# Attention loads paced along the preceding batch, last six outputs scaled by ScalarE, and a replanned order

## The chip, the cores and the metric

The kernel runs on one core of a Trainium2 chip. The core has five engines that run side by side, each with its own queue of instructions: TensorE (PE, matrix products; its weight loads are shown as PEld), VectorE (DVE), ScalarE (ACT), GpSimd (POOL) and SyncE (SP), which here only issues DMAs. The metric is device time in microseconds of one execution; less is better.

## What is computed

Block-sparse attention for 4 batches, 8 heads, 768 positions and 64 channels a head, followed by a two-layer block over the 3072 rows of 512 channels:

```python
scores = scale * np.matmul(q, k.transpose(0, 1, 3, 2))
scores = np.where(mask, scores, -1000000000.0)      # first, last, neighbour and sampled blocks
attn = np.exp(scores - max) / sum
x = (attn @ v), rows (batch, position), columns (head, channel)
h = x @ w_in                                         # 512 -> 1024
solu = h * softmax(h)
ln = (solu - mean) / np.sqrt(var + 1e-06) * g_ln
out = ln @ w_out                                     # 1024 -> 512
```

## The kernel before

The mask enters as 24 further channels of queries and keys (one for each block of 32 positions), so that one matrix product of 88 channels gives masked scores. Scores are computed with the keys along the partitions; the row sum of the exponentials comes out of the value product through a column of ones in `va`.

**Attention.** A unit is (batch b, tile t of 256 queries, pair pr of heads): 4 x 3 x 4 = 48 units. Each has three groups of four score matmuls (`score`, L495) into a PSUM bank group `sbank`, three exponentials on ScalarE (L502) into `ex`, three groups of eight value matmuls (`pv`, L512) into one of two small banks `mbank`, and on VectorE a reciprocal (L523) and a scaling (L526) into `x`. There are three `sbank`s; from batch 1 on, two serve scores and one the dense layers.

**Feed.** When the four pairs of a tile are done, its 256 rows go through the dense layers in two halves a = 0, 1. `x` is transposed (by a DMA transpose on SP, L556, or by TensorE for the first and last tile), then: eight matmuls with `w_in` (`hmm`, L567), an exponential with row sums on ScalarE (L576), the product h * exp on VectorE (L580, called `so`), centring (L584, `ce`), statistics (L587, L590), an inverse root on GpSimd (L592 to L598), a transpose of the centred rows (L606, or by TensorE), eight matmuls with `w_out` (`outp`, L613) into an `mbank`, a scaling of the result by the inverse root (`fin`, L623) into `ot`, and a store on SP (L629).

**Loads.** Keys, queries and values come in by pairs of heads, 384 KB a load, on SP (`load`, L270), into four staging buffers each. From batch 1 on, keys and queries are cast on GpSimd (L417), transposed by a DMA on SP (L422) and copied to `kT` and `qT` by VectorE (L427); values are cast by GpSimd (L477). Loads, transposes and stores all stand on the one queue of SP, in order: a transpose that waits for its cast holds back every load behind it.

**The order.** No loop issues the work. Every piece is made as an `Op` with an engine, an assumed duration, what it depends on (`deps`), what it must merely be planned after (`after`), buffers to take, and a due time; lists `A` (units), `F` (feeds), `Q` (preparation of heads) and `SHIFT` hold the due times. `Plan.run` then lays all ops out on the engines with a model of durations and DMAs, and the program is emitted in that order. On the chip only the order on each engine's queue is kept, and the waits that the data call for. The plan's own times are not used in what follows.

Of the kernel before, what the change touches and what calls it, by code (L numbers as in the profile page):

```python
# [12 lines left out]
ACT = mybir.ActivationFunctionType  # L13
# [9 lines left out]
def act_us(n, sbuf=False):  # L23
    return (n + 60 + (52 if sbuf else 0)) / 1200
# [31 lines left out]
class Plan:  # L56


    def __init__(self):
        self.ops = []  # L60
        self.pools = {}
        self.free = {e: 0.8 for e in SEEN}
        self.dma_free = 0.0
        self.xbar_free = 0.0
        self.landed = []

    def pool(self, name, n, of=None, first=0):
# [3 lines left out]
    def op(self, eng, us, emit, deps=(), due=0.0, take=None, last_of=(), load=None, after=()):  # L71
        o = Op(eng, us, emit, deps, due, take, last_of, load, after)
        for d in {id(d): d for d in o.deps + o.after}.values():
            d.next.append(o)
            o.open += 1
        for a, name in o.last_of:
            a.held[name][0] += 1
        self.ops.append(o)
        return o

    def run(self):
        ready = {e: [] for e in SEEN}

        def enter(o):
            o.at = max([0.0] + [d.seen for d in o.deps] + [d.start for d in o.after])
            ready[o.eng].append(o)

        for o in self.ops:
            if not o.open:
                enter(o)  # L90
        order = []
        while len(order) < len(self.ops):
            best = None
            for e, ops in ready.items():
                now = self.free[e]
                for o in ops:
                    t = o.at
                    for name in o.take:
                        free, ids = self.pools[name]
                        t = max(t, min(free[k] for k in ids))  # L100
                    if t == INF:
                        continue
                    late = t > now + 0.02
                    key = (t if late else now, o.due)
                    if best is None or key < best[0]:
                        best = (key, o, max(t, now))
            assert best is not None, "nothing can be placed"
            _, o, t = best
            ready[o.eng].remove(o)
            us = o.us * (2 if o.eng == "PE" and t < COLD else 1)  # L110
            self.free[o.eng] = t + us
            o.start = t
            o.seen = t + us + SEEN[o.eng]
            if o.load is not None and o.xbar:
                self.xbar_free = max(self.xbar_free, t + 1.0) + o.load * (1.4 if self.dma_free > t + 1 else 1.0)
                self.dma_free = max(self.dma_free, t) + o.load
                o.seen = self.xbar_free + 1.3
            elif o.load is not None and o.eng != "SP":
                o.seen = t + (2.8 if o.load > 0.1 else 2.0) + o.load + 0.6 * min(o.load, max(0.0, self.dma_free - t - 1.5))
                if o.load > 0.1:  # L120
                    self.dma_free = max(self.dma_free, t + 1.5) + o.load
            elif o.load is not None:
                self.dma_free = max(self.dma_free, t + 1.0) + o.load
                o.seen = self.dma_free + 1.0
                self.landed.append(self.dma_free)
                if len(self.landed) > 6:
                    self.free["SP"] = max(t + o.us, self.landed[-7])
            for name in o.take:
                free, ids = self.pools[name]
                o.slots[name] = min(ids, key=lambda k: (free[k], k))  # L130
                free[o.slots[name]] = INF
            for a, name in o.last_of:
                held = a.held[name]
                held[0] -= 1
                held[1] = max(held[1], o.seen)
                if not held[0]:
                    self.pools[name][0][a.slots[name]] = held[1]
            order.append((t, len(order), o))
            for n in o.next:
                n.open -= 1  # L140
                if not n.open:
                    enter(n)
        order.sort(key=lambda r: r[:2])
        return [o for _, _, o in order]
# [3 lines left out]
def kernel(  # L148
# [13 lines left out]
    B, H, S, D = q.shape  # L162
# [7 lines left out]
    NPR = H // 2  # L170
# [57 lines left out]
    plan = Plan()  # L228
# [5 lines left out]
    plan.pool("h", 1, "sh", 2)  # L234
    op = plan.op
    LOAD = 2 * P * NCH * D * 4 / 330e3
    TILE = 0.023

    def bank(o, dt=FP32):
        t = mbank[o.slot]  # L240
# [6 lines left out]
        return sbank[o.slot].rearrange("p a b -> p (a b)")  # L247

    def xbar_us(tiles):
        return 1.35 if tiles < 64 else 1.5  # L250


    samp_i = const.tile([NB, NR, 2], I32, name="samp_i")
# [11 lines left out]
    stage, loads = {}, []  # L265
# [40 lines left out]
    mid, stz, last = fill(ident, 0.0, -2198), fill(static, 0.0, -2197), fill(anyeq, 0.0, -2196)  # L306

    def sel(t, us, fill, base, cm, pat, deps, cmp=ALU.is_ge):
# [7 lines left out]
            due=-2194)  # L316
# [8 lines left out]
    for r in range(NR):  # L325
        last = op("DVE", 0.24, lambda o, r=r: nc.vector.scalar_tensor_tensor(
            out=anyeq, in0=kbi, scalar=samp_i[:, r, 0:1], in1=anyeq, op0=ALU.is_equal, op1=ALU.max),
            [last, io, samp_dma], due=-2089)
# [3 lines left out]
    def selq_tr(o):  # L332
        for c in range(NCH):
# [5 lines left out]
             due=-2189, last_of=[sqt])  # L339
# [5 lines left out]
               due=-2079.6)]  # L345
# [24 lines left out]
    for i in (1, 2, 0):  # L370
# [8 lines left out]
                due=-1900 if i == 0 else 0) for i in range(2)]  # L379
# [5 lines left out]
    w_out_load = []  # L385
    for i in range(3):
        w_out_load.append(op("SP", 0.5, lambda o, i=i: nc.sync.dma_start(
            out=hold[i], in_=moe_w_out.rearrange("(c p) d -> p c d", p=P)[:, 3 * i : min(3 * i + 3, KF)]),
            due=-43.4 + 0.1 * i, load=2.3, deps=w_in_load[:1], after=[stage[("v", 0, 3)]] + w_out_load[-1:]))
    stage[("k", 1, 0)].after.append(w_out_load[-1])  # L390
    w_out_load[-1].next.append(stage[("k", 1, 0)])
    stage[("k", 1, 0)].open += 1
    gt = op("PE", 0.1, lambda o: nc.tensor.matmul(bank(o)[:, 0:KF], g8, identf[0:KF, 0:KF], start=True, stop=True),
            [g_load, idf, stage[("k", 0, 2)]], due=15, take="m")
    gc = op("DVE", 0.1, lambda o: nc.vector.tensor_copy(out=g_sb, in_=bank(gt)[:, 0:KF]), [gt], due=15,
            last_of=[gt])
# [88 lines left out]
    def attend(b, t, pr, A):  # L485
# [4 lines left out]
        for n in range(3):  # L490
            def score(o, n=n):
                s = sbank[o.slot]
                for m in range(4):
                    hh, jc = divmod(4 * n + m, NCH)
                    nc.tensor.matmul(s[:, m, :], kT[i][0:DM, pr, hh, jc * P : (jc + 1) * P],  # L495
                                     qT[i][0:DM, pr, hh, t * TW : (t + 1) * TW],
                                     start=(m % 2 == 0), stop=(m % 2 == 1))

            so = op("PE", 4 * 0.1087, score, need[0] + (need[1] if n else []), due=A + 0.9 * n,
                    take="sh" if b == 0 and t < 2 else "s")  # L500
            last_use.setdefault((b, pr), []).append(so)
            exs.append(op("ACT", act_us(1024), lambda o, so=so: nc.scalar.activation(  # L502
                out=exb[o.slot], in_=sbank[so.slot], func=ACT.Exp, scale=scale), [so], due=A + 0.9 * n,
                take="ex", last_of=[so]))
        pv0 = None
        for n in range(3):
            def pv(o, n=n, pv0=pv0):
                acc = bank(pv0 or o)[:, 0 : 4 * (D + 1)].rearrange("p (a h d) -> p a h d", a=2, h=2)
                for m in range(4):
                    hh, jc = divmod(4 * n + m, NCH)  # L510
                    for qt in range(2):
# [6 lines left out]
                     last_of=[exs[n]], after=[pv_last] if n else [])  # L518
# [12 lines left out]
            take="x" if fresh else None, last_of=[pv0, rc])  # L531
# [17 lines left out]
    def feed(b, t, F, by_pe, late):  # L549
# [10 lines left out]
        for a in range(2):  # L560
            h0 = None
            for n in range(4):
                def hmm(o, n=n, h0=h0, a=a):
                    h = pair(h0 or o)
                    f = n // 2
                    for c in (2 * (n % 2), 2 * (n % 2) + 1):
# [5 lines left out]
                       take=None if n else ("sh" if late else "h"), last_of=[xp] if n == 3 else [],  # L572
# [10 lines left out]
                last_of=[h0, (se, "e")])  # L583
# [14 lines left out]
            rs = op("POOL", 0.55, lambda o, mv=mv: nc.gpsimd.tensor_tensor(  # L598
                out=rsb[o.slot], in0=mvb[mv.slot][:, 0:1], in1=neg_half, op=ALU.pow), [q2, nh],
                due=F[a] - 30, take="rs", last_of=[mv])  # L600
# [24 lines left out]
                else:  # L625
                    nc.scalar.activation(out=otb[o.slot], in_=bank(o0), func=ACT.Copy, scale=rsb[rs.slot])

            fo = op("DVE", 0.74, fin, [om, rs], due=F[a] + 7, take="ot", last_of=[o0, rs])
            op("SP", 0.45, lambda o, a=a, fo=fo: nc.sync.dma_start(  # L629
                out=out_v[b, 2 * t + a], in_=otb[fo.slot]), [fo], due=F[a], last_of=[fo], load=0.8)  # L630

# [1 line left out]
    units += [(b, t, pr) for b in range(1, B) for t in range(NT) for pr in range(NPR)]  # L633


    A = [-45.65, 40.00, 223.39, 84.45, 113.83, -10.10, 148.66, 400.63, 32.23, 154.32, 246.42, 58.30, -154.55,
         -261.32, -38.68, -86.73, -83.04, -37.93, -122.58, -397.07, -7.44, 96.20, 125.06, 92.18, -24.08,
         -186.30, 68.39, -9.13, -331.82, 0.92, 45.16, -14.53, -5.50, 84.85, 136.68, 26.21, 15.45, 11.53,
         -92.83, -240.79, 14.95, 126.21, -14.78, 139.91, -324.93, 225.39, 184.04, 142.76]
    F = [-252.59, -78.30, 47.15, -69.94, -182.12, -193.82, 100.11, -114.06, 22.11, -50.57, -74.19, -53.05,  # L640
         275.34, -203.17, 194.98, -23.42, -88.40, 56.44, 21.43, 55.08, 340.35, 167.71, 248.37, 18.28]
    Q = [-252.59, 107.13, -181.40, 669.66, 579.50, 93.95, 204.07, 225.32, 34.97, -16.48, 130.68, -51.20,
         -335.57, -838.94, -885.84, -745.64]
    for b in range(B):
        for pr in range(NPR if b == 1 else 0):

# [11 lines left out]
            j = b * NT + t  # L658
            feed(b, t, F[2 * j : 2 * j + 2], j in (0, B * NT - 1), j >= B * NT - 3)

    SHIFT = {"score": -3.8, "hmm": 113.54, "outp": 336.1, "pv": -218.66}
    for o in plan.ops:
        o.due += SHIFT.get(o.emit.__name__, 0.0)

# [42 lines left out]
```

## Time and profile before

| | |
|---|---|
| Median of 13 runs | 214.19 us (212.82 to 219.13) |
| The profiled execution, its own time | 212.82 us |
| Its span, from first to last instruction | 210.8 us |
| DMA | 41.28 MB, mean 196 GB/s |
| Exponentials of attention (L502) | 144, 1043 ns each, 137.2 us in all |
| Scalings of the output (L623) | 24, 748 ns each, 18.0 us in all |
| Products of the dense layer (L580) | 24, 1222 ns each, 29.3 us in all |
| Landing of a load of keys, queries, values | 5.1, 5.4, 4.5 us (median) |
| Landing of a DMA transpose of keys, queries, x, centred rows | 4.2, 3.9, 3.6, 3.7 us (median) |

The busy times of the engines overlap. Matmuls are pipelined, so a matmul's own duration in the table of groups is longer than the time from one to the next. In a few places a matmul's record is missing from the trace; weight loads are complete, and the starts of blocks are read from them.

### The profile page before, as it was taken

What the parts mean: (1) busy time and instruction counts of PE and PEld (TensorE: products, weight loads), DVE (VectorE), ACT (ScalarE), POOL (GpSimd) and SP (SyncE); (2) the same over time, 40 slices, a digit from 0 to 9 for tenths busy, and PEclk for the clock granted to TensorE, in tenths of its full rate; (3) what the DMA queues carried; (4) which work ended last, traced back from release to release, by engine and by line L of the source; (5) the groups of instructions that cost most, each with busy time, mean ns of one, the idle gap of its engine ahead of it and who ended that gap; (6) DMA issues with size and microseconds to landing.
All of it is one profiled execution on the core that took longest, in us unless ns stands there. A gap on an engine that the chain in (4) does not pass through costs nothing.

```text
span 210.8 us, 5781 instructions
## 1 busy us (share of the span) xinstructions
PE 198.6 (94%) x2269; PEld 141.6 (67%) x2298; DVE 161.9 (77%) x379; ACT 165.6 (79%) x202; POOL 63.4 (30%) x131
## 2 busy tenths in 40 slices
PE   7899999989999999999999999999999999999981
PEld 6589878857667777666677777667665566644430
DVE  4797998747995986985856675894848797789882
ACT  6699999988998899999799889699955688743000
POOL 5143026333642462246243111233011112121120
PEclk9999999999999999999999999999999999999999
DMA  5999998999999998999999952543674755325522
GB/s 176 317 384 344 263 314 210 214 260 279 257 207 214 301 235 174 306 206 331 227 317 237 245 98 65 89 115 87 96 158 100 127 124 101 96 50 155 151 103 100
DMA packets 69119, 41.28 MB, mean 196 GB/s; under 512 B 52188, under 2 KB 64484, under 8 KB 69092
## 3 DMA queue, kind: packets, MB, share of 16 engines
q1 hardware_dynamic: 68496, 39.86, 77.0%
q0 software_dynamic: 544, 1.05, 2.6%
q8 instruction: 18, 0.29, 0.6%
q14 instruction: 9, 0.07, 0.1%
q10 hardware_dynamic: 52, 0.00, 0.0%
HBM read 23.07 MB, written 6.29 MB: 139 GB/s over the span
## 4 chain that ended last, share of the span: by engine, by line
PE 74%; ACT 10%; DVE 4%; DMA 4%; issue 3%; SPq 2%; POOL 0%; ACTq 0%; DVEq 0%; POOLq 0%
PE sbank L495 24%; PE mbank L613 17%; PE sbank L567 17%; PE mbank L512 13%; ACT ex L502 10%; DMA kb<-kb 2%; DMA qst<-in_q_dram 2%; SPq L270 2%; DVE ot L623 1%; PE mbank L459 1%; DVE kT L427 1%; PE mbank L542 1%; DVE bn L587 1%; ACT eso L576 0%; DVE qT L427 0%
## 5 line engine op out<-in xcount | busy, mean ns | idle before, releaser
L502 ACT ACTIVATE ex<-sbank 128x1024 bf16<-128x1024 f32 x144 | 137.2, 1043 | 11.6 <-PE sbank L495 10.8
L495 PE MATMUL sbank<-qT,kT 88*128 88x256 bf16 x576 | 81.8, 272 | 3.2 <-ACT ex L502 2.1
L495 PEld LDWEIGHTS <-kT 88*128 88x128 bf16 x576 | 52.6, 97 | 23.7 <-issue 7.2
L567 PE MATMUL sbank<-w_in_sb,xT 128*128 128x512 bf16 x174 | 47.9, 379 | 0.8
L613 PE MATMUL mbank<-w_out_sb,eso 128*128 128x512 bf16 x181 | 45.6, 379 | 1.7 <-DVE ot L623 1.2
L512 PEld LDWEIGHTS <-ex 128*128 128x128 bf16 x1152 | 42.4, 98 | 6.6 <-DVE x L526 0.2
L512 PE MATMUL mbank<-va,ex 128*128 128x65 bf16 x1152 | 44.0, 193 | 0.1
L580 DVE SCALAR_TENSOR_TENSOR eso<-sbank,eso 128x1024 bf16<-128x1024 f32 x24 | 29.3, 1222 | 10.8 <-ACT eso L576 10.8
L576 ACT ACTIVATE eso<-sbank 128x1024 bf16<-128x1024 f32 x24 | 24.8, 1031 | 15.3 <-issue 3.1
L587 DVE BATCH_NORM_STATS2 bn<-eso 128x6 f32<-128x512 bf16 x48 | 30.7, 682 | 0.2
L613 PEld LDWEIGHTS <-eso 128*128 128x128 bf16 x192 | 18.3, 97 | 18.1 <-issue 1.6
L567 PEld LDWEIGHTS <-xT 128*128 128x128 bf16 x192 | 18.3, 98 | 11.3
L594 POOL TENSOR_SCALAR mv<-se,mv 128x1 f32<-128x1 f32 x24 | 6.9, 288 | 60.3 <-DVE mv L590 54.6
L523 DVE RECIPROCAL r<-mbank 128x4 f32<-128x4 f32 x48 | 8.3, 174 | 17.9 <-PE mbank L512 17.7
L623 DVE TENSOR_SCALAR ot<-mbank,rs 128x512 f32<-128x512 f32 x24 | 18.0, 748 | 5.0 <-PE mbank L613 4.2
L526 DVE TENSOR_TENSOR x<-mbank,r 128x256 bf16<-128x256 f32 x48 | 20.0, 418 | 0.8
L477 POOL CAST va<-vst 128x768 bf16<-128x768 f32 x16 | 13.2, 826 | 16.7 <-DMA vst<-in_v_dram 11.8
L598 POOL TENSOR_TENSOR rs<-mv,neg_half 128x1 f32<-128x1 f32 x24 | 13.9, 579 | 13.0 <-DVE ot L623 11.8
L417 POOL CAST kb<-kst 128x768 bf16<-128x768 f32 x12 | 10.5, 872 | 15.6 <-ACT ex L502 10.7
L417 POOL CAST qb<-qst 128x768 bf16<-128x768 f32 x12 | 10.8, 898 | 12.9 <-DMA qst<-in_q_dram 10.6
L427 DVE COPY kT<-kb 64x768 bf16<-64x768 bf16 x24 | 10.5, 436 | 3.7 <-DMA kb<-kb 2.9
L584 DVE TENSOR_SCALAR eso<-eso,mu 128x1024 bf16<-128x1024 bf16 x24 | 13.2, 548 | 0.1
(72 smaller groups left out, 97.8 us busy)
## 6 DMA issues: line engine op xcount, KB each, us to landing
vst<-in_v_dram SPq DMA_DIRECT2D x16, 384.0 KB, 4.5
out_dram<-ot SPq DMA_DIRECT2D x24, 256.0 KB, 2.3
kst<-in_k_dram SPq DMA_DIRECT2D x15, 384.0 KB, 5.1
qst<-in_q_dram SPq DMA_DIRECT2D x15, 384.0 KB, 5.4
w_in_sb<-in_moe_w_in_dram POOLq DMA_DIRECT2D x2, 512.0 KB, 11.5
kT<-in_moe_w_out_dram SPq DMA_DIRECT2D x1, 768.0 KB
qT<-in_moe_w_out_dram SPq DMA_DIRECT2D x1, 768.0 KB, 16.1
eso<-in_moe_w_out_dram SPq DMA_DIRECT2D x1, 512.0 KB
```

What stands on the lines that cost most here:

```text
L417: nc.gpsimd.tensor_copy(out=half(cb[o.slot], 0).rearrange("p (c h d) -> p c h d", c=NCH, h=2), in_=st[ld.slot].rearrange("p h c d -> p c h ...
L495: nc.tensor.matmul(s[:, m, :], kT[i][0:DM, pr, hh, jc * P : (jc + 1) * P], qT[i][0:DM, pr, hh, t * TW : (t + 1) * TW], start=(m % 2 == 0), ...
L502: exs.append(op("ACT", act_us(1024), lambda o, so=so: nc.scalar.activation(out=exb[o.slot], in_=sbank[so.slot], func=ACT.Exp, scale=scale) ...
L512: nc.tensor.matmul(acc[:, qt, hh, :], exb[exs[n].slot][:, m, qt * P : (qt + 1) * P], va[i][:, 2 * pr + hh, jc, :], start=(n + m + qt == 0) ...
L526: nrm = op("DVE", 0.41, lambda o: nc.vector.tensor_tensor(out=xb[x_of[(b, t)].slot][:, :, 2 * pr * D : (2 * pr + 2) * D].rearrange("p a (h ...
L567: nc.tensor.matmul(h[:, f * 512 : (f + 1) * 512], xTb[xp.slot][:, a, c, :], w_in_sb[:, c, f * 512 : (f + 1) * 512], start=(c == 0), stop=( ...
L576: se = op("ACT", act_us(d_ff) + 0.22, lambda o, h0=h0: nc.scalar.activation(out=eb[o.slots["e"]], in_=pair(h0), func=ACT.Exp, accum_out=se ...
L580: so = op("DVE", 1.3, lambda o, h0=h0, se=se: nc.vector.scalar_tensor_tensor(out=sob[o.slot], in0=pair(h0), scalar=1.0, in1=eb[se.slots["e ...
L587: bn = op("DVE", 2 * 0.68, lambda o, so=so: [nc.vector.bn_stats(out=bnb[o.slot][:, f], in_=sob[so.slot][:, f * 512 : (f + 1) * 512]) for f ...
L598: rs = op("POOL", 0.55, lambda o, mv=mv: nc.gpsimd.tensor_tensor(out=rsb[o.slot], in0=mvb[mv.slot][:, 0:1], in1=neg_half, op=ALU.pow), [q2 ...
L613: nc.tensor.matmul(bank(o0 or o), sotb[st.slot][:, f, :], w_out_sb[:, f, :], start=(f == 0), stop=(f == KF - 1))
L623: nc.vector.tensor_scalar(out=otb[o.slot], in0=bank(o0), scalar1=rsb[rs.slot], scalar2=None, op0=ALU.mult)
```

## The change

Four things. In the model of the plan, DMA transposes and loads share one DMA queue, where transposes had one of their own, and SP is held up by them in another way; the assumed costs of a transpose change with it. Each load of batches 2 and 3 is planned after the first score group of one unit of the batch before (twelve loads, twelve units). The scaling of the last six outputs is given to ScalarE. And the due times `A`, `F`, `Q` and `SHIFT` are new, so that the order differs on every engine from the first blocks on. The instructions are otherwise the same ones, with the same shapes.

```diff
+    def follow(self, o, d):
+
+        o.after.append(d)
+        d.next.append(o)
+        o.open += 1
...
-            if o.load is not None and o.xbar:
-                self.xbar_free = max(self.xbar_free, t + 1.0) + o.load * (1.4 if self.dma_free > t + 1 else 1.0)
-                self.dma_free = max(self.dma_free, t) + o.load
-                o.seen = self.xbar_free + 1.3
-            elif o.load is not None and o.eng != "SP":
+            if o.load is not None and o.eng != "SP":
...
             elif o.load is not None:
-                self.dma_free = max(self.dma_free, t + 1.0) + o.load
-                o.seen = self.dma_free + 1.0
+
+                before, last = self.dma_free, self.xbar_seen
+                self.dma_free = max(before, t + 1.0) + o.load
+                o.seen = self.dma_free + 0.9
                 self.landed.append(self.dma_free)
+                if o.xbar:
+                    self.free["SP"] = max(t + us, last - 1.5, before - 4.0)
+                    self.xbar_seen = o.seen
...
-    TILE = 0.023
+    TILE = 0.0245
...
-        return 1.35 if tiles < 64 else 1.5
+        return 1.24
...
             last_use.setdefault((b, pr), []).append(so)
+            if n == 0 and 1 <= b < B - 1:
+
+                l = NPR * t + pr
+                plan.follow(stage[("kqv"[l % 3], b + 1, l // 3)], so)
...
-            fo = op("DVE", 0.74, fin, [om, rs], due=F[a] + 7, take="ot", last_of=[o0, rs])
+            fo = op("ACT" if late else "DVE", 0.52 if late else 0.74, fin, [om, rs], due=F[a] + 7, take="ot", last_of=[o0, rs])
...
-    A = [-45.65, 40.00, 223.39, 84.45, 113.83, -10.10, 148.66, 400.63, 32.23, 154.32, 246.42, 58.30, -154.55,
+    A = [51.93, 316.63, -115.93, 231.11, 59.19, -252.77, -562.27, -274.63, -180.24, 25.80, 75.07, -201.10,
...
-    SHIFT = {"score": -3.8, "hmm": 113.54, "outp": 336.1, "pv": -218.66}
+    SHIFT = {"score": 83.14, "hmm": 360.52, "outp": 460.27, "pv": -613.9}
```

`late` is true for the three tiles of batch 3, two outputs each. `fin` already held both branches: a multiplication on VectorE, or `nc.scalar.activation` with `Copy` and the inverse root as scale.

## The prediction

> **What bounds the kernel now.** I read the page's engine shares first, then the busy time by windows, then the chain that ended last in order of time, then the timeline of the last stretch. One execution is shown: span 210.8 us, its own time 212.82 us, so 2.0 us lie around the span; the median of 13 runs is 214.19, or 1.4 us more.
>
> Page, shares of the engines:
> ```profile
> PE 198.6 (94%) x2269; PEld 141.6 (67%) x2298; DVE 161.9 (77%) x379; ACT 165.6 (79%) x202; POOL 63.4 (30%) x131
> ```
> Windows (busy us and instruction counts of PE, weight loads, DVE, ACT, POOL; clock; DMA share; GB/s):
> ```profile
> 20.00:30.00 10.00, 9.81 (x154) 8.64 (x153) 8.81 (x22) 10.00 (x12) 0.00 (x0) 1.00 1.08 301
> ...
> 90.00:100.00 10.00, 9.45 (x109) 6.67 (x109) 6.86 (x17) 9.58 (x14) 5.42 (x9) 1.00 1.18 272
> ...
> 130.00:140.00 10.00, 9.89 (x101) 6.68 (x102) 8.39 (x20) 8.13 (x11) 2.49 (x6) 1.00 0.36 57
> ```
> TensorE is busy everywhere at full clock; ScalarE is full only early; the DMA engines are full to about 120 us and a third busy later. A share of 94% does not say how much of TensorE's time is necessary, so I priced its blocks from the dense rows of the chain (start, us, what):
> ```profile
> 17.44 0.75 PE mbank L512 x24
> 18.19 0.88 PE sbank L495 x8
> ...
> 147.41 1.73 PE mbank L613 x8
> ...
> 191.65 1.73 PE sbank L567 x8
> ```
> Dense, a score matmul costs 0.109 us, a value matmul 0.031, a matmul of the two dense layers 0.216, a transpose 0.056. So 576 x 0.109 + 1152 x 0.031 + 384 x 0.2156 + 48 x 0.056 is 183.8, and some 4.6 for the transposes of batch 0: 188.4 us of necessary work. The first score starts at 8.2 and the last matmul ends at 206.4, which is 198.2. TensorE lost about 9.7 us in between, and these alone are to be had, apart from the 4.4 after the last matmul.
>
> To place the loss I took each block's start less 8.1 less the necessary work ahead of it ("lag"). It is 5.0 us at 48 us, 5.6 at 61, 5.9 at 67, 6.7 at 99, 7.1 at 105, 7.85 at 180 and 9.4 at 203. Three causes:
> - To 61 us, ScalarE. It runs 144 exponentials in 137.2 us, 0.953 each, and a score cannot reuse a PSUM bank before its exponential is done. Adding the exponentials up in order against the TensorE work ahead of the first block that needs them, the worst place of the old order is 43 x 0.953 + 1 x 1.24 (an exponential of the dense layer, 1.03 + 0.21) = 42.2 against 37.0 of work: 5.3 us behind. Measured 5.0; VectorE adds the rest by 61.
> - At 99 us, 0.8 us, and 0.3 when it restarts: a late transpose on the queue of SyncE.
> ```profile
> 89.94 0.58 SPq L270
> ...
> 90.57 1.55 SPq L270
> ...
> 92.17 0.47 SPq L270
> ...
> 92.74 4.86 DMA kb<-kb
> ...
> 97.62 0.36 DVE kT L427
> ```
> The last keys of batch 2 wait on SP behind three loads of batch 3 (2.6 us, one stuck 1.55), then 4.86 us for a transpose whose usual landing is 4.2.
> - In the last 15 us, 1.6 us: VectorE holds the two small PSUM banks.
> ```profile
> 201.92 0.75 DVE L623 TENSOR_SCALAR ot<-mbank,rs 128x512 f32<-128x512 f32 x1 [0.25 <-issue]
> 202.59 0.20 DVE L590 BATCH_NORM_AGGREGATE mv<-bn 128x2 f32<-128x12 f32 x1
> 202.71 0.64 DVE L546 COPY eso<-mbank 128x1024 bf16<-128x1024 bf16 x1
> 202.73 3.61 PE L613 MATMUL mbank<-w_out_sb,eso 128*128 128x512 bf16 x16 [0.90 <-DVE ot L623]
> ```
>
> **What the Trainium skill says.** "Perfetto Trace Analysis", Identifying the Most-Contended Engine: matmul occupancy is no measure of headroom, weight-load share is a better one. The trace agrees: 94% against 67%; hence the sum above. "DMA: Bandwidth & Descriptors", Anatomy of one DMA: semaphore waits sit on the issuing sequencer, the DMA engines wait for none; and under Issuing engines are not separate DMA queues: all issuers share the same 16 engines. Both are seen: the rows at 89.94 to 92.74, and queue q1 with 39.86 of 41.28 MB. "ScalarE: Activation LUTs", Table sets: copy is in every table set. The trace has one table load although copies (L342, L354, L467) and exponentials share the engine, so six Copy activations between exponentials should bring none.
>
> **The change part by part.** The count of instructions per engine is the same but for six scalings; all else is order.
>
> 1. New order in the first 60 us. At 48.3 us of work the new order has 53 attention and 3 dense exponentials due: 53 x 0.953 + 3 x 1.24 = 54.2, so 6.0 behind, where the old peak was 5.3. VectorE's own queue, summed the same way from the first product of the dense layer on, asks for 1.5 us beyond its start in the old order and 1.0 in the new. Taking both, lag at 53 us of work is about 6.0 against 5.9 measured before: +0.1, ends 0 and +0.9 (the two shortfalls add up fully).
>
> 2. Pacing. It adds no semaphore: it only sets where a load stands on SP's queue. Counted from the built order, a load of keys or queries of batch 2 or 3 stands at least 20.9 us of TensorE work ahead of the first score that needs it. What it needs: landing 5.4, cast 0.9, issue 1.24, transpose landing 4.2, two copies 0.87, near 12.6. Values have 11.9 and more against 4.5 + 0.83. So the loads are not late, though they now stand behind two transposes and stores of outputs, which wait for VectorE. The transposes of the last keys of batch 2 now stand behind two other transposes and no load, with 10.3 us against 2 x 1.24 + 1.24 + 4.2 + 0.87 = 8.8. The 0.8 + 0.3 stall should go: -1.1, ends -1.1 and 0. Last loads go out nearer 125 us than 115.7; DMA there is idle enough. What is late next: VectorE at 112.8 us of work (0.4 by its queue's sum) and the transpose for batch 3, tile 1 (5.1 us against 0.7 + 3.6 + waits). I take +0.2, ends 0 and +0.8.
>
> 3. Six scalings on ScalarE. They take 6 x 0.748 = 4.5 us off VectorE's last 30 us, where it is 90% busy from 180 to 200, and put them on an engine with 2.2 us of work in 190 to 200 and none after. No row shows a 512-column Copy; between a 256-column copy (0.365) and a 1024-column exponential (1.03), 512 columns give about 0.59; the skill's rule under Rules for kernel authors (0.3 us and 0.83 ns an element) gives 0.73. I take 0.6: the very last scaling gets 0.15 shorter (ends 0 and 0.2). Inside the tail I walked the new order with the durations above: the copy of the first transposed block waits for VectorE, and the scaling of output (3, 2, 0) on ScalarE waits for its inverse root, since its aggregate stands on VectorE behind the last product (1.3 us) and GpSimd adds 0.27 + 0.55 and hops. That bank is wanted by the last transpose. The walk gives 1.7 to 1.9 of stall; the same kind of sum for the old tail gives 2.6 where 1.6 was measured, so it overstates by 1. I take 1.1 against 1.6: -0.5, ends -1.6 and +0.4. Without ScalarE's cover, VectorE would owe the 4.5 us again in the same place.
>
> Sum: +0.1 - 1.1 + 0.2 - 0.5 - 0.15 = -1.45, so 211.4 against 212.82 in its own execution, and 212.7 against the median.
>
> **Rivals.**
> - A deeper gain: the front costs nothing, the tail stall all but goes (-1.6), nothing new appears: -1.1 - 1.6 - 0.15 = -2.85, 211.3. For it: ScalarE lies idle in the tail. Against it: the wait for the inverse root.
> - No change: ScalarE's extra 0.7 at the front stays on, VectorE's 0.4 and the tail at 1.9 appear as summed: +0.7 - 1.1 + 0.4 + 0.3 - 0.15 = +0.15, 214.3. For it: every later stall can only add to a lag that the front already set.
> - Slower: paced loads late. Each store and transpose on SP waits for VectorE, and a load behind it waits along. If that holds a load back by more than the spare 20.9 - 12.6 = 8.3 us, the pair of heads it belongs to starts late. The one late pair above cost 1.1 with its restart; four pairs would cost 4.4 less the gain of 1.45: +2.9, 217.1; three give 216.0. For it: SP waited 12.3 us for VectorE ahead of stores. Against it: the longest single wait there was 3.3 us. I take 216.0 for it.
> - The pacing does nothing: the old queue already trickled its loads out to 115.7 us as buffers came free. Then the gain is that of order alone and falls within the first two cases.
>
> **How the numbers follow.** Forecast 212.7, chance 0.45, its own range 211.7 to 213.5. Deeper gain 0.13. No change 0.20. Slower 0.22. About 0.3%, 0.64 us, is what measurement can tell from no change. Forecast and deeper gain lie below 213.55 but for a little at the edge: faster 0.57; same 0.20; slower 0.23. The range takes in the deeper gain and most of the slower case, and half a microsecond for the scatter of medians: 210.9 to 215.9.
>
> **What would show it.** Lag near 6 us at 60 us of time, as before; no gap on TensorE near 99 us and no transposed keys for which VectorE idles; DMA busy to about 125 us at lower shares; scalings on ScalarE near 0.6 us and no second table load; 1 us or so of gaps in the last 15 us, the last of them ahead of the final transpose. It is wrong if VectorE idles for landed transposes or GpSimd's casts wait for loads in batches 2 and 3, or if ScalarE's lag passes 7 us.

## The result, and the profile after

| | before | after |
|---|---|---|
| Median, run side by side | 214.35 us (212.75 to 220.05, 48 runs) | 211.11 us (210.43 to 214.23, 11 runs) |
| Profiled execution, own time | 212.82 us | 211.43 us |
| Its span | 210.8 us | 209.7 us |
| Time around the span | 2.0 us | 1.7 us |

The ratio of the two is 0.9861, with a 95% interval of 0.9839 to 0.9884: the change takes 1.4% off, about 3.0 us. Ratios here and below leave out disturbed executions, those well above the fastest of their kernel, so a ratio can differ a little from that of two medians. Between the two profiled executions the difference is 1.39 us. Both figures are needed below: the forecast was worked out on the second and carried over to the first.

The page of after, shares of the engines, and its DMA row of 40 slices (tenths, each slice 5.2 us):

```profile
PE 199.0 (95%) x2270; PEld 141.5 (67%) x2298; DVE 157.8 (75%) x373; ACT 169.9 (81%) x208; POOL 63.6 (30%) x131
...
DMA  5999997979994086998989989999790464634522
```

Six instructions went from VectorE to ScalarE: 4.1 us less on the one, 4.3 us more on the other. From the 2nd slice on the DMA engines stay at seven tenths or more to the 30th, 157 us, where the forecast said about 125. The exception is the 13th to the 16th slice, 63 to 84 us, with 4, 0, 8 and 6 tenths: between 54 and 76 us no load goes out.

The same windows as before the change (busy us and counts of PE, weight loads, DVE, ACT, POOL; clock; DMA share; GB/s):

```profile
20.00:30.00 10.00, 9.79 (x144) 8.49 (x142) 8.40 (x20) 10.00 (x12) 0.00 (x0) 1.00 1.09 297
90.00:100.00 10.00, 9.83 (x124) 7.40 (x126) 7.20 (x19) 8.59 (x11) 3.52 (x6) 1.00 1.10 223
130.00:140.00 10.00, 9.89 (x142) 7.43 (x141) 8.11 (x19) 8.75 (x12) 4.54 (x9) 1.00 1.17 261
```

From 90 to 100 us TensorE is busy 9.83 us where it was 9.45: the stall near 99 us is gone. From 130 to 140 us the DMA share went from 0.36 to 1.17 and TensorE did not lose by it: these are the loads that are now paced into the second half.

The last stretch, from the timeline of after (start, us, engine, line, operation):

```profile
201.35 0.69 ACT L635 ACTIVATE ot<-mbank,rs 128x512 f32<-128x512 f32 x1 [1.04 <-PE mbank L622]
...
202.08 0.61 PE L551 MATMUL mbank<-ident,eso 128*128 128x128 bf16 x8
...
202.53 2.92 PE L622 MATMUL mbank<-w_out_sb,eso 128*128 128x512 bf16 x12
202.80 0.69 DVE L555 COPY eso<-mbank 128x1024 bf16<-128x1024 bf16 x1 [0.98 <-PE mbank L551]
```

The scaling of `ot` on ScalarE runs beside VectorE's work, the final transposes start at 202.08 as it ends, and `outp` of the tile before goes on under the copy of the transposed block. No row of TensorE there has an idle time of its own; before, `outp` waited 0.90 us for VectorE's scaling.

With the measure of the prediction, lag (a block's start less the first score's and the necessary work ahead of it), the two profiles compare like this:

| us | before | after | difference |
|---|---|---|---|
| First score starts | 8.11 | 7.75 | -0.36 |
| Lag at 50 us of work | 5.82 | 7.13 | +1.31 |
| Growth, 50 to 180 us of work | 1.87 | 1.45 | -0.42 |
| Growth, 180 to 188 us of work | 1.72 | 0.29 | -1.43 |
| From the last block's start to the end | 5.24 | 5.03 | -0.21 |
| Sum | | | -1.11 |

That is the 1.1 us between the spans; the other 0.3 lies around them. The front got worse by far more than expected, the tail got better by far more, and the middle by less.

The table rests on one execution of each kernel. In two further profiles of the kernel before, the stall in the middle is much larger than the 0.8 us of the first; this is shown with the experiments.

### The profile page after: what moved, and what is told of

The parts are those of the page before. It is cut to its first block, busy times and chain, and to the rows that moved or that the text cites. A ratio compares the mean times of both kernels' runs of the same rounds, so it can differ in the third digit from the quotient of the medians.

```text
span 209.7 us, 5779 instructions
## 1 busy us (share of the span) xinstructions
PE 199.0 (95%) x2270; PEld 141.5 (67%) x2298; DVE 157.8 (75%) x373; ACT 169.9 (81%) x208; POOL 63.6 (30%) x131
## 2 busy tenths in 40 slices
DMA packets 69119, 41.28 MB, mean 197 GB/s; under 512 B 52188, under 2 KB 64484, under 8 KB 69092
## 3 DMA queue, kind: packets, MB, share of 16 engines
q1 hardware_dynamic: 68496, 39.86, 77.1%
## 4 chain that ended last, share of the span: by engine, by line
PE 76%; ACT 11%; DMA 4%; SPq 3%; issue 3%; DVE 2%; ACTq 0%
PE sbank L500 24%; PE mbank L622 19%; PE sbank L576 17%; PE mbank L521 14%; ACT ex L511 9%; DMA kst<-in_k_dram 4%; SPq L277 3%; PE mbank L551 1%; ACT eso L585 1%; DVE w_out_sb L403 1%; PE mbank L464 1%; DVE qT L472 0%; ACT ot L635 0%; DVE kb L446 0%; DVE x L535 0%
## 5 line engine op out<-in xcount | busy, mean ns | idle before, releaser
L500 PE MATMUL sbank<-qT,kT 88*128 88x256 bf16 x576 | 82.9, 272 | 2.5 <-ACT ex L511 1.9
L576 PE MATMUL sbank<-w_in_sb,xT 128*128 128x512 bf16 x177 | 48.6, 379 | 0.6
L521 PEld LDWEIGHTS <-ex 128*128 128x128 bf16 x1152 | 41.7, 97 | 6.6 <-issue 1.4
L521 PE MATMUL mbank<-va,ex 128*128 128x65 bf16 x1152 | 43.1, 193 | 1.2 <-DVE qT L472 0.7
L589 DVE SCALAR_TENSOR_TENSOR eso<-sbank,eso 128x1024 bf16<-128x1024 f32 x24 | 29.3, 1221 | 10.2 <-ACT eso L585 10.0
L585 ACT ACTIVATE eso<-sbank 128x1024 bf16<-128x1024 f32 x24 | 24.8, 1033 | 15.0 <-PE sbank L576 10.5
L603 POOL TENSOR_SCALAR mv<-se,mv 128x1 f32<-128x1 f32 x24 | 7.4, 309 | 61.4 <-DVE mv L599 52.1
L482 POOL CAST va<-vst 128x768 bf16<-128x768 f32 x16 | 13.8, 863 | 17.2 <-DMA vst<-in_v_dram 17.0
L632 DVE TENSOR_SCALAR ot<-mbank,rs 128x512 f32<-128x512 f32 x18 | 13.5, 748 | 4.0 <-PE mbank L622 3.0
L422 POOL CAST kb<-kst 128x768 bf16<-128x768 f32 x12 | 10.5, 873 | 15.6 <-PE mbank L521 10.7
L601 POOL TENSOR_TENSOR se<-se 128x1 f32<-128x1 f32 x24 | 4.8, 200 | 32.1 <-ACT eso L585 32.1
L422 POOL CAST qb<-qst 128x768 bf16<-128x768 f32 x12 | 10.2, 852 | 8.0 <-DMA qst<-in_q_dram 6.5
L593 DVE TENSOR_SCALAR eso<-eso,mu 128x1024 bf16<-128x1024 bf16 x24 | 12.3, 513 | 0.3
```

Source lines behind the costliest of these rows:

```text
L422: nc.gpsimd.tensor_copy(out=half(cb[o.slot], 0).rearrange("p (c h d) -> p c h d", c=NCH, h=2), in_=st[ld.slot].rearrange("p h c d -> p c h ...
L482: vc = op("POOL", pool_us(S) + 0.3, lambda o: nc.gpsimd.tensor_copy(out=va[i][:, 2 * pr : 2 * pr + 2, :, 0:D], in_=vst[ld.slot]), [ld, von ...
L521: nc.tensor.matmul(acc[:, qt, hh, :], exb[exs[n].slot][:, m, qt * P : (qt + 1) * P], va[i][:, 2 * pr + hh, jc, :], start=(n + m + qt == 0) ...
L576: nc.tensor.matmul(h[:, f * 512 : (f + 1) * 512], xTb[xp.slot][:, a, c, :], w_in_sb[:, c, f * 512 : (f + 1) * 512], start=(c == 0), stop=( ...
L585: se = op("ACT", act_us(d_ff) + 0.22, lambda o, h0=h0: nc.scalar.activation(out=eb[o.slots["e"]], in_=pair(h0), func=ACT.Exp, accum_out=se ...
L589: so = op("DVE", 1.3, lambda o, h0=h0, se=se: nc.vector.scalar_tensor_tensor(out=sob[o.slot], in0=pair(h0), scalar=1.0, in1=eb[se.slots["e ...
```

## Experiments

Three questions: which part of the change brings the gain; why the gain between typical executions (3.0 us) is twice that between the two profiled ones (1.4 us); and whether the rival in which paced loads come late is real.

### The kernel before, profiled again

No edit.

> The kernel before, unchanged, profiled a second time. Its first profile was of its fastest execution (212.82 us, median 214.35). Theory A (the typical execution loses more to transposes and loads that land late while the DMA engines are full): an execution near 214.3 us shows a lag some 1 to 1.5 us higher than the first profile's by 110 us of the span, and more waits of VectorE or GpSimd for DMAs. Theory B (the typical execution has a lower TensorE clock): lag grows evenly over the span, granted clock under 1.00, waits for DMAs as before. Theory C (it is lost outside the span): span 210.8 again.

> The kernel before, a third profile. Theory A: whatever its time, the lag added between 80 and 92 us of TensorE work differs from execution to execution (1.1 us in the first profile, near 5 with a dip of the clock in the second), and in an execution near 214.3 us it is 2 us or more. Theory B: it is 1.1 us again and the difference to 212.8 us lies in the first 15 us or in the clock.

Measured: 221.98 us (span 219.9) and 217.9 us (span 215.9), one execution each. Windows of the second (columns as above), and its TensorE timeline around 100 us:

```profile
97.00:100.00 3.00, 3.00 (x32) 2.04 (x29) 1.22 (x3) 2.88 (x4) 1.65 (x2) 1.00 1.09 338
100.00:103.00 3.00, 0.74 (x6) 0.36 (x4) 1.79 (x6) 1.75 (x4) 1.50 (x3) 0.98 0.94 215
103.00:106.00 3.00, 3.00 (x32) 2.17 (x31) 1.80 (x4) 1.14 (x2) 1.20 (x3) 0.50 0.99 255
```

```profile
99.87 0.38 PE L495 MATMUL sbank<-qT,kT 88*128 88x256 bf16 x2
102.50 0.38 PE L495 MATMUL sbank<-qT,kT 88*128 88x256 bf16 x2 [2.26 <-DVE qT L427]
```

The stall that was 0.8 us in the first profile is a gap of 2.26 us here, and TensorE's clock then stands at 0.50 for 3.41 us. Between 80 and 92 us of work the lag grows by 4.5 us, against 1.12 in the first profile. The first of the two repeats shows the same gap with 2.28 us at 104.2 us and the same half clock, 5.0 us of lag in all; it had also run at half clock from 9.0 to 19.3 us, at its start. What follows: the stall that the change removes varies from execution to execution, and 212.82 us was an execution with a small one. The front varies too: before 50 us of work the second repeat lost some 2 us more than the first profile, at full clock. Over the 69 further executions of the kernel before whose mean clock is 0.994 or more (a stretch of 3.4 us at half clock would leave 0.992), the median is 213.95 us (212.97 to 216.37), 1.1 us above the one profiled first.

Both repeats lie well above that median, so they do not give the size of the stall in a typical execution.

### The stall at 99 us read again

The two repeats show scores (L495) waiting for queries, `qT`, where the prediction had named late keys. VectorE's timeline of the kernel before settles it:

```profile
94.26 0.35 DVE L427 COPY qT<-qb 64x768 bf16<-64x768 bf16 x1
94.53 1.27 DVE L587 BATCH_NORM_STATS2 bn<-eso 128x6 f32<-128x512 bf16 x2
97.62 0.73 DVE L427 COPY kT<-kb 64x768 bf16<-64x768 bf16 x2 [1.81 <-DMA kb<-kb]
98.38 0.21 DVE L590 BATCH_NORM_AGGREGATE mv<-bn 128x2 f32<-128x12 f32 x1
98.62 0.36 DVE L427 COPY qT<-qb 64x768 bf16<-64x768 bf16 x1
```

VectorE idles 1.81 us for a transposed block of keys. These are not the last keys of batch 2 but the first of batch 3, which no score wants yet. Behind their two copies stands one copy of queries of batch 2, pair 3, which have landed (the other half of them was copied at 94.26), and the scores at 99.03 wait for that. So TensorE waits for the place of an instruction on VectorE's queue, and the late transpose only makes VectorE's wait long.

### That copy moved ahead

```diff
+    at = {id(o): i for i, o in enumerate(order)}
+    first = ready[3, 0][0][0][0]
+    at[id(ready[2, 3][0][1][1])] = at[id(first)] - 0.5
+    order.sort(key=lambda o: at[id(o)])
```

in the kernel before, ahead of the loop that emits the order.

> The kernel before with one VectorE instruction moved: the copy of the second half of the queries of batch 2, pair 3 stands ahead of the two copies of the first keys of batch 3, which wait for a late transpose. Theory E (the stall near 99 us is VectorE's order: landed queries stuck behind keys that are not there): 0.8 to 1.1 us faster than before, 213.3 to 213.5, no gap near 99 us. Theory A (the transposes are late because loads fill the DMA engines, and the first scores of batch 3 need those keys 4 us of work later anyway): 0 to 0.5 us faster, and the wait turns up at those scores in a disturbed execution.

Measured: 214.31 us, ratio 0.9943 (0.9907 to 0.9979). Its chain of waits (start, us, what):

```profile
93.47 5.13 DMA kb<-kb
...
98.63 0.36 DVE kT L427
...
99.00 0.36 DVE kT L427
...
99.68 0.43 DVE x L526
...
100.16 0.93 PE mbank L512 x24
```

The scores go through now, but the next that stands behind the same two copies, the scaling into `x` (L526), holds up the value products: TensorE idles 0.58 us ahead of them. The stall moved to the next victim. In the profile the lag between 80 and 92 us of work grows by 1.27 against 1.12, so that nothing is gained there; the ratio says about 0.6% for the typical execution. That is inconclusive on the size; it does show that VectorE still waits, and that the wait finds another victim, as long as the transpose is late.

### The copy moved and the transpose put ahead of two loads

```diff
+    flip = first.deps[0]
+    for n, o in enumerate((stage["v", 3, 0], stage["k", 3, 1])):
+        at[id(o)] = at[id(flip)] + 0.1 + 0.1 * n
```

added to the edit before: two of the three loads of batch 3 stand on SP behind the transpose instead of ahead of it.

> As b_swap, and two of the three loads of batch 3 that stand ahead of that transpose on SP's queue (values of pair 0, keys of pair 1) stand behind it. If this one place is what pacing cures, theory A expects most of the change's 3 us: 1.5 to 2.5 us faster than before, about 212.3. If the loads disturb in many places (theory F), this one edit gives 0.5 to 1.2 us, 213.2 to 213.8.

Measured: 216.19 us, ratio 1.0016 (0.9965 to 1.0066): nothing gained, less than either theory expected. The gap at 99 us is gone from the profile, and one of 1.27 us ends at 104.84, at the first scores of batch 3, which wait for `qT` and so for a transpose that landed after 5.65 us. Of the four transposes of keys and queries issued between 89 and 102 us, three took 5.65 to 6.42 us to land. Repairing this one place by hand does not pay; that the loads have to leave the whole stretch is the conclusion that the next experiment tests.

### The loads at their old places, in the kernel after

```diff
+    for k, o in enumerate(loads[-24:]):
+        held = max(held, at[id(loads[-25])], spot[id(o)], done_at[k])
+        at[id(o)] = min(at[id(o)], held + 0.5)
+    order.sort(key=lambda o: at[id(o)])
```

`done_at` holds the place in the order at which as much TensorE work is done as stood ahead of each of the 24 loads of batches 2 and 3 before the change (26.4 us for the first, 94.6 for the last); `spot` is where its staging buffer comes free.

> The changed kernel with one thing undone: each load of batches 2 and 3 stands on SP's queue where the kernel before has it, counted in TensorE work ahead of it (26 to 95 us instead of 33 to 113). Everything else keeps its order. Theory A (pacing keeps the DMA engines free for transposes): 1 to 2 us slower than the changed kernel, about 212.5, and gaps on TensorE or VectorE behind transposes between 50 and 110 us. Theory D (the gain is the tail and the new order, pacing buys nothing): within 0.5 us of the changed kernel's 211.1.

Measured: 214.63 us, ratio 0.9992 (0.9961 to 1.0023). All of the gain is gone. From the chain of waits of its profile (an execution of 216.37 us, so above its median):

```profile
96.16 1.60 SPq L277
...
97.85 0.42 SPq L277
...
98.84 5.31 DMA kb<-kb
...
104.18 0.35 DVE kT L432
```

The picture of the kernel before is back: loads ahead of a transpose on SP, one of them stuck 1.60 us, then a slow landing. TensorE shows gaps of 1.69 us at 60.9, 1.08 at 98.1 and 0.71 at 106.2. VectorE waits 8.0 us in five places for transposed keys and 2.6 us in three for queries; in the profile of after it is 0.2 and 0.3 us, one place each. Which of the two does the harm, the place behind loads on SP's queue or the slow landing beside them, no run separates.

### The six scalings on VectorE, in the kernel after

```diff
+    for o in order:
+        if o.emit.__name__ == "fin":
+            o.eng = "DVE"
```

> The changed kernel with the last six scalings on VectorE, at the same places in the order. Theory D (the tail carries about half of the gain, through ScalarE): 1.0 to 1.5 us slower than the changed kernel, 212.1 to 212.6, with the stalls of TensorE back in the last 15 us. Theory A: the tail would be nearly as good by its order alone, 0.2 to 0.5 us slower.

Measured: 212.49 us, ratio 0.9940 (0.9912 to 0.9969), 0.8% above after. In its profile lag grows by 1.46 us from 180 to 188 us of work, where after has 0.29 and before 1.72. From its timeline:

```profile
204.36 0.75 DVE L632 TENSOR_SCALAR ot<-mbank,rs 128x512 f32<-128x512 f32 x1
...
205.16 0.61 PE L551 MATMUL mbank<-ident,eso 128*128 128x128 bf16 x8 [0.56 <-DVE ot L632]
...
206.94 1.25 PE L622 MATMUL mbank<-w_out_sb,eso 128*128 128x512 bf16 x5 [0.32 <-DVE eso L555]
```

The last transposes wait for the scaling to give the bank back, and `outp` waits for the copy behind it: VectorE owes both again, as the prediction had said it would without ScalarE's cover.

### The six scalings on ScalarE, in the kernel before

```diff
+            def fin_late(o, fin=fin):
+                o.eng = "ACT"
+                fin(o)
...
-            fo = op("DVE", 0.74, fin, [om, rs], due=F[a] + 7, take="ot", last_of=[o0, rs])
+            fo = op("DVE", 0.74, fin_late if late else fin, [om, rs], due=F[a] + 7, take="ot", last_of=[o0, rs])
```

The order is as before; only the engine is another.

> The kernel before with its last six scalings on ScalarE, at the same places in the order. Theory D: the tail stall of 1.6 us shrinks to 0.5 or less, 213.0 to 213.3 against 214.35. Theory A: the tail's order, not the engine, made the stall, and it stays over 1 us: 213.9 to 214.3.

Measured: 214.88 us, ratio 0.9979 (0.9946 to 1.0012): no clear gain, and growth in the tail 1.65 us against 1.72. Its timeline:

```profile
209.45 0.69 ACT L626 ACTIVATE ot<-mbank,rs 128x512 f32<-128x512 f32 x1 [1.52 <-PE mbank L613]
...
210.19 2.10 PE L613 MATMUL mbank<-w_out_sb,eso 128*128 128x512 bf16 x9 [0.82 <-ACT ot L626]
```

The 0.90 us of waiting for VectorE turned into 0.82 us for ScalarE: here the next `outp` wants the bank as soon as it is written, and the scaling waits for its inverse root, whichever engine does it. The free engine pays only with the new order. That it does so because other matmuls stand between there is read from the timelines and was not tried apart.

### Both parts undone: the new order alone

The edits of the last two kernels made from after, together.

> The changed kernel with both parts undone: loads of batches 2 and 3 at their old places and the last six scalings on VectorE; only the order of everything else is new. If the parts add up (oldpos cost 1.3% and dve 0.8%), 0.8% slower than before, near 216. If they overlap, 0 to 0.4% slower than before.

Measured: 216.88 us, ratio 1.0079 (1.0046 to 1.0112). With after this makes a table of four, all as change against the kernel before, each good to some 0.3%:

| | scalings on VectorE | scalings on ScalarE |
|---|---|---|
| Loads at old places | +0.8% | -0.1% |
| Loads paced | -0.6% | -1.4% |

The new order by itself costs 0.8% (1.7 us). Pacing brings 1.4% in the left column (0.994 less 1.0079, or 3.0 us of 214) and 1.3% in the right one; ScalarE brings 0.9% (1.9 us) above and 0.8% below. The parts add up: +1.7, -2.9 and -1.8 make -3.0 us. What the first row leaves open: a part of the 1.7 us may come from the old places of the loads fitting the new order worse than the one they were made for.

### Loads half way, and loads later still

The edit of the loads at old places, with the mean of old and new places (twice, the second time beside after), and from after, each load put back by another 4.0 us of TensorE work, though never behind its cast:

```diff
+    for o in loads[-24:]:
+        late = next((i for i, w in enumerate(when) if w >= when[at[id(o)]] + 4.0), len(order))
+        need = min(at[id(d)] for d in o.next if d.eng == "POOL")
+        held = max(held, at[id(o)], min(late, need - 1) + 0.5)
+        at[id(o)] = held
```

> The changed kernel with the loads of batches 2 and 3 half way between their old and their new places. Theory F (each load pulled forward adds DMA traffic in the full stretch before 110 us): between the changed kernel and a_oldpos, 212 to 213.5. Theory G (a threshold: only the earliest places hurt): within 0.5 us of 211.1.

> The changed kernel with the loads of batches 2 and 3 another 4 us of TensorE work later where their cast allows it. Theory F: the same as the changed kernel or up to 0.5 us faster, since spare time is still 16 us of work. The prediction's slower rival (loads late) would show here first: over 1 us slower, with GpSimd's casts waiting for loads and TensorE for keys.

> The changed kernel with the loads half way between old and new places, beside the changed kernel itself. Theory G (a plateau between too early and too late): within 0.5 us of it. If more spare time helps, 0.3 to 1 us faster, and it is the best version.

> The changed kernel itself, beside a_half2 on the same chip: 211.1, about 1.4% under before.

| Loads | Median | Ratio |
|---|---|---|
| old places | 214.63 | 0.9992 (0.9961 to 1.0023) |
| half way | 211.23 | 0.9823 (0.9768 to 0.9877) |
| half way, second time | 211.06 | 0.9835 (0.9799 to 0.9871) |
| as in after, beside the second | 212.39 (6 runs) | 0.9868 (0.9814 to 0.9922) |
| 4.0 us later | 220.77 | 1.0260 (1.0201 to 1.0320) |

The intervals of half way and after overlap both times: between them the place makes no difference that the runs can tell, so no version is shown to beat after. Another 4 us of work later the whole gain is lost, and the time is 2.6% above that of the kernel before. The waits of that kernel (total us, times, longest):

```profile
POOL va L482 <- DMA vst<-in_v_dram: 35.4, 10, 8.8
...
POOL kb L422 <- DMA kst<-in_k_dram: 14.9, 7, 3.5
...
POOL qb L422 <- DMA qst<-in_q_dram: 10.4, 5, 5.1
DVE qT L432 <- DMA qb<-qb: 10.3, 5, 3.2
```

and the same rows in after:

```profile
POOL va L482 <- DMA vst<-in_v_dram: 17.0, 11, 4.2
...
POOL qb L422 <- DMA qst<-in_q_dram: 6.5, 6, 2.2
...
POOL kb L422 <- DMA kst<-in_k_dram: 4.5, 6, 2.0
```

GpSimd's casts wait for loads, then VectorE for transposes, then TensorE: gaps of 1.80 us at 68.5, 1.59 at 96.6 and 1.82 at 104.9. This is the way of the queries of batch 2, pair 2, from their load to their first scores (rows of the timelines of SP, GpSimd, VectorE and TensorE):

```profile
95.12 0.47 SPq L277 DMA_DIRECT2D qst<-in_q_dram  x1
...
100.10 0.82 POOL L422 CAST qb<-qst 128x768 bf16<-128x768 f32 x1
...
101.21 2.02 SPq L427 DMA_TRANSPOSE qb<-qb  x1
...
106.30 0.33 DVE L432 COPY qT<-qb 64x768 bf16<-64x768 bf16 x1
...
106.68 1.05 PE L500 MATMUL sbank<-qT,kT 88*128 88x256 bf16 x8 [1.82 <-DVE qT L432]
```

They take 11.6 us, with the scores waiting for them. In after the same load goes out at 84.89 and the first weight load of its scores starts at 101.49, 16.6 us later. With loads and scores paired by the order in which the kernels emit them, the queries of batch 2 go out 10.2 to 12.4 us ahead of their first scores here and 15.4 to 18.1 us in after; the values of three of its four pairs go out 4.4 to 5.6 us ahead of their value products here and 9.0 to 12.3 us in after. So the rival that ended slower is a real mechanism, and after stands one step of 4 us from it.

## Why the prediction was right, and where its steps were off

The forecast for the profiled execution, -1.45 us, met -1.39; the forecast of the median, 212.7, was 1.6 us too high, with 211.11 near the fast end of its range of 210.9 to 215.9. Both have to be taken apart: the first came so close by luck, through errors that cancel.

- **The first 60 us: +0.1 was forecast, +1.31 - 0.36 = +0.95 measured in the profiles.** Just outside the end of +0.9 that was kept. The step that failed is the sum of ScalarE's durations: 54.2 us of exponentials against 48.3 us of work was to give a lag of 6.0 us, and it is about 7 there. The sum takes ScalarE never to idle. In the timeline of after it idles 0.90 us, since TensorE waited 0.71 us at 17.4 for a copy of queries behind a cast of late-landing keys (`kst`, 9.32 us in the chain):

```profile
19.93 12.94 ACT L511 ACTIVATE ex<-sbank 128x1024 bf16<-128x1024 f32 x14 [0.90 <-PE sbank L500]
```

  But this idle time is not what the new order costs. In the second profile of after (210.87 us) ScalarE does not have it:

```profile
16.76 17.66 ACT L511 ACTIVATE ex<-sbank 128x1024 bf16<-128x1024 f32 x19 [0.34 <-PE sbank L500]
```

  and still the lag at 50 us of work is only 0.2 us lower. All eight profiles of the new order have a gap of 1.03 us on TensorE that starts between 45 and 50 us, where scores wait for an exponential; here in after and in its second profile:

```profile
47.48 0.60 PE L500 MATMUL sbank<-qT,kT 88*128 88x256 bf16 x4 [1.03 <-ACT ex L511]
...
46.73 0.60 PE L500 MATMUL sbank<-qT,kT 88*128 88x256 bf16 x4 [1.03 <-ACT ex L511]
```

  The lag grows by 1.2 us there; in the kernel before the largest single growth near that work is 0.8 us. That the new order costs something is confirmed by the +0.8%; what makes up the cost stays open.
- **The middle: -1.1 + 0.2 was forecast; -0.42 between the profiles, and by the runs the largest term, -2.9.** The mechanism is shown: undo the pacing and the gain goes. Between the two profiles the stall itself went as forecast: lag between 80 and 92 us of work grows by 1.12 us before and by 0.14 after. What was short there is the term of +0.2: at 113 us of work the lag of after grows by 0.48 us at once, where scores wait for an exponential; the prediction had looked for VectorE there. The stall's place was right, its reading in part wrong: the waiting scores wanted queries held behind keys of batch 3 on VectorE, not the last keys of batch 2. Its size was off for the median, because the stall was taken from the one execution in which it was small: 1.12 us of lag there, 4.5 and 5.0 in two others. And the pacing was priced at this one stall, while the loads at old places make several, at 61, 98 and 106 us.
- **The tail: -0.5 - 0.15 forecast, -1.43 - 0.21 measured in the profiles, 1.7 to 1.9 us by the runs.** The mechanism was right; the walk was held back by the scaling that waits for its inverse root. That scaling came in time (201.35, the transposes at 202.08), so that of the 1.1 us of remaining stall 0.29 is left, near the end of -1.6 that was kept. The Copy itself was put at 0.6 us and took 0.687; the prediction's other price, from "ScalarE: Activation LUTs", Rules for kernel authors, gave 0.73 and was nearer. One line of groups has it:

```profile
L635 ACT ACTIVATE ot<-mbank,rs 128x512 f32<-128x512 f32 x6 | 4.1, 687 | 7.8 <-PE mbank L622 4.4 <-issue 2.3 <-POOL mv L603 1.0
```

- **The carry-over: the constant 1.4 us from own execution to median failed.** It is the step that put the median 1.6 us too high. For the kernel before, the distance from the profiled execution to the median of the later runs is 1.5 us; for after it is -0.3. So the gap was no constant of the chip's. Its likeliest cause is the stall that the change takes away, which was small in the execution profiled first; a rival is the front, which differed by some 2 us between two profiles of the kernel before. This is argued from the two repeats and the spread; no profile of a full-clock execution of about 214 us was taken, so the last 1 us is not placed.
- **The slower rival: its mechanism is real, and less time was to spare than it reckoned.** The need of 12.6 us from load to first score was about right: 10.2 to 12.4 us were measured for queries whose scores came late. The lead was not: by its place in the queue a load of keys or queries was to stand at least 20.9 us of work ahead, and in the trace of after queries go out 15.4 us ahead at the least. So some 3 us were to spare, not 8.3, and with the loads 4 us later the time was 2.6% above that of the kernel before.
- **The rival that pacing does nothing** falls: loads at the old places lose all of the gain.
- **The deeper gain** (211.3) is nearest to the median measured, but not by its reasons: it had the front at nothing and no difference between executions.

The signs that were named: no gap near 99 us, hardly any idle time of VectorE for landed transposes (0.5 us), no second table load, short stalls in the tail, all seen. Lag near 6 us at 60 us: wrong, it was 6.9 there and 7.1 at 50 us of work. DMA busy to 125 us: to 157. Two of the signs that were to show it wrong came up as well: the lag passed 7 us, and GpSimd's casts waited for loads of batches 2 and 3, from 50 to 150 us of after for 4.2, 4.0 and 3.6 us (values, queries, keys). The second was no good sign: in the kernel before the same waits, from 48 to 125 us, come to 10.5 us.

Two readings of the trace in the prediction do not hold. It took 94% against 67% to agree with the weight-load share as the better measure; its own sum makes 188.4 of 210.8 us necessary, 89%, which is nearer to the share of the matmuls. And the 39.86 of 41.28 MB on queue q1 say how much one queue carried, not that all issuers share the same engines.

## What to carry to other kernels

Profile the kernel before several times before pricing a stall: here the same stall cost 1.1 us of lag in one execution and 4.5 and 5.0 in two others. Where loads share one issuing queue with transposes that are needed soon, spread the loads over the stretch in which there is slack, and count their lead from the time at which they really go out, not from their place in the order: here 15.4 us was enough for queries, and 10 to 12 was not. Work moved to an idle engine paid here only in an order that lets its consumer wait; look for that before moving it.

## What was not expected of the hardware

TensorE fell to half clock in the middle of kernels in which it is 92 to 94% busy, after gaps of 2.28, 2.26 and 1.82 us, each time for 3.4 us. Two windows of the kernel with loads later still (columns as above):

```profile
105.00:107.70 2.70, 1.02 (x8) 0.70 (x8) 2.62 (x9) 1.49 (x4) 0.00 (x0) 1.00 1.03 208
107.70:111.10 3.40, 3.39 (x53) 3.17 (x53) 2.38 (x7) 1.63 (x2) 0.71 (x1) 0.50 0.92 279
```

No such dip followed gaps of 1.80, 1.69 or 1.59 us. A dip costs about 1.7 us more, half of its length, so that by this count a stall of 2.3 us costs 4. The Trainium skill, "TensorE: Matmul & The Clock Gate", Why this matters for your kernels, advises against idle gaps above some 3 us; here 1.82 was enough. Its section What's actually happening speaks of a free-running window of about 3.4 us, which agrees with the length of the dips, and would let the phase of a gap decide as much as its length: 1.80 and 1.82 us lie too close for a threshold.

The traces bear this out in the middle of the kernels. In the first repeat the clock changes at 9.03, 19.27, 108.02 and 111.43 us, 3, 26 and 1 times 3.413 us apart, and in the other profiles, too, all changes lie on such a grid. Of the grid's windows, two of those ahead of a dip (the second repeat; the loads later still) and two with a long gap but no dip after it (the loads later still; the loads at old places):

```profile
99.49:102.91 3.42, 1.16 (x8) 0.57 (x6) 1.70 (x6) 2.25 (x4) 1.90 (x4) 1.00 1.00 224
104.29:107.71 3.42, 1.60 (x11) 0.78 (x9) 3.31 (x11) 2.21 (x4) 0.00 (x0) 1.00 1.00 221
...
66.75:70.16 3.41, 1.75 (x32) 1.20 (x29) 0.27 (x1) 2.17 (x3) 0.24 (x1) 1.00 1.10 171
59.56:62.98 3.42, 1.73 (x22) 1.02 (x21) 1.25 (x4) 3.09 (x5) 1.06 (x3) 1.00 1.12 123
```

TensorE is busy 1.16 and 1.60 us of the first two, less than half, and 1.75 and 1.73 us of the others, a little over half. So the idle time within a window, and not the length of a gap, sorts these cases; more of them would be needed for a rule. At the start and the end of a kernel it does not sort them: a window with 2.04 us busy was followed by a dip (the first repeat, at 5.62), while windows with 2.02 us (the copy moved and the transpose put ahead, at 4.17) and with 1.53 us (the second profile of after, at 203.37) were not. Half clock at the start of five of the profiled executions lasted 6.8, 6.8, 10.2, 10.2 and 13.7 us, two to four such windows.
